# Block 0's k and q from row loads of their own, in a fused window attention and squared-ReLU feed-forward kernel

## The chip, the cores and the metric

The kernel runs on one core of a Trainium2 chip. A core has a matrix engine (TensorE, "PE" in the profile; its weight loads are "PEld"), a vector engine (VectorE, "DVE"), a scalar engine for activations (ScalarE, "ACT"), a general engine (GpSimd, "POOL"), and a queue engine (SyncE, "SP") that here issues nearly all DMA transfers. All five run programs of their own and wait for one another through semaphores. The metric is device time in microseconds (us), less is better; times of a kernel are the median of several runs.

## What is computed

```python
def _attn_ref(q, k, v):                      # each (8, 8, 576, 64): batch, heads, seq, head_dim
    scores = (1.0 / np.sqrt(64)) * np.matmul(q, k.transpose(0, 1, 3, 2))
    pos = np.arange(576)
    mask = np.abs(pos[:, None] - pos[None, :]) <= 32
    scores = np.where(mask, scores, -1000000000.0)
    scores = scores - np.max(scores, axis=-1, keepdims=True)
    attn = np.exp(scores)
    attn = attn / (np.sum(attn, axis=-1, keepdims=True) + 1e-09)
    return np.matmul(attn, v)

def _moe_ref(x, w_in, w_out, s, b):          # x (4608, 512), w_in (512, 2048), w_out (2048, 512)
    r = np.maximum(x @ w_in, 0.0)
    return (s * (r * r) + b) @ w_out
```

The attention's output, with the heads joined to rows of 512, is the feed-forward part's input x: 8 x 576 = 4608 tokens. Everything arrives as float32; the matrix products run in bfloat16.

## The kernel before

The 4608 tokens are 36 blocks of 128. A block's queries look at keys from 32 tokens before it to 32 behind it. For every block the attention makes a tile XT (the block's output, transposed), and the feed-forward part works on tiles of TILES: ten of 128 tokens, then thirteen of 256.

**Feed-forward.** For each tile, groups of 16 matmuls (L1188) make 512 columns of the hidden layer in the bank HT[0] or HT[1]; ACT or DVE takes the ReLU (L1197), DVE squares it into GT (L1216). Then four quarters of 4 matmuls each (L1238) add up the output in OUTP or PTPF, in turn; a quarter needs a quarter of w_out. The factor s and the constant b times w_out's column sums come in at L1252; those sums, cvec, are made once by PE from the whole of w_out (L1077).

**Attention.** Blocks 0 and 1 go through attend_light: scores for a group of four heads, in SC[0] or SC[1] (mask L800, products L810), a maximum for each query (L868), the same scores transposed (L800, L824) corrected by that maximum (L873, L875, L831, L836), one exponential (L892), the product with v (L845 to L852), scaling (L902, L904), a transpose back (L912) and the copy to XT. With NSPLIT = 1 block 0's two groups are heads 0 to 3 and heads 4 to 7, so that the first group needs only the first half of k and q. All other blocks go through attend: scores (L950), mask, minimum and exponential head by head (L962, L970), normalisation (L976 to L984), a transpose of the probabilities (by PE up to block 4, L1007, later by DMA), and the product with v (L1029 or L1046). A block j needs v tiles j and j + 1 (VE, VO).

**Where k and q come from.** For blocks 0 to 3 (WHOLE = 4) they come from whole-batch loads: "K0", "K1", "Q0", "Q1" (load_raw) bring batch 0 of k and q, four heads each, as 128 rows of 4608 bytes into RAW, which borrows space in GT. turn_raw casts them in four pieces each to FLAT, PE turns them by the permutation PERM (L691), and the banks are copied into TURN["K"] and TURN["Q"], from which keys(j) and qs(j) read. From block 4 on k and q come in tiles of 256 tokens ("k2", "q4" and so on, load_k and load_q), are cast (cast_kq) and transposed (kq_turn, L768).

**The weights.** w_in comes in four chunks i0 to i3 of 512 hidden columns, w_out in four chunks o0 to o3, each 1 MB in float32, into staging slots (SLOT: 0 to 3 lie in GT, 4 in OUTA), and each is cast in four pieces to WIN and WOUT (load_w, cast). v tiles are "v0", "v1" and so on (load_v, cast_v, make_vo).

**What sets the order.** All loads stand in one chain on SP, in the order of the string FIRST ("|" marks the block behind which the rest is put); each load stands behind the one before. Everything else is ordered by a planner (class _Plan): each operation is a node with a set of engines that it may run on, a cost, and a key; the planner walks through a model of the five engines and gives each engine the ready operation with the least key. What it finds is fixed in the program: an engine runs its list in that order and waits where an operand isn't there. Where PE would be idle early on, it puts in matmuls that compute nothing ("warm", L567; the first seven L571). akey(j) is the key of block j's attention, set by LEAD, L0 and LS; ckey gives the casts of loads their keys from their places in FIRST and from CB. LOOK, LOOK_GAP and LOOK_END would let an engine wait a moment for an operation that is due. FLEX, CSET, VSET, OSET and WSET say which engines may do which copies and casts, NSQ for how many blocks of tokens POOL may square.

```python
    FIRST = "Q0 Q1 K0 K1 i0 v0 v1 i1 i2 v2 i3 q4 v3 o0|k2 q5 v4 o1 o2 o3 v5||||"
    SLOT = dict(i0=0, i1=1, i2=2, i3=3, o0=0, o1=4, o2=1, o3=0)
    def akey(j):
        return 128 * j - min(LEAD, L0 + LS * j)
```

## Time and profile before

| | |
|---|---|
| median of 3 runs (lowest, highest) | 316.08 us (315.13, 317.0) |
| the profiled execution: its time | 316.29 us |
| its span from first to last instruction | 314.4 us |
| granted TensorE clock, mean over the span | 1.000 |
| DMA moved | 61.56 MB, mean 196 GB/s |
| most PE time: L1188 (hidden layer) | 147.1 us busy, 1472 matmuls |
| L1238 (output), the banks outp and ptp | 68.1 and 64.4 us busy |
| most DVE time: L1216 (square) | 82.0 us, 144 of 571 ns |
| most ACT time: L970 (exponential) | 113.3 us, 272 of 421 ns |
| most POOL time: L984 (normalisation) | 71.9 us, 64 of 1141 ns |

The profile is that of one execution. Its rows give an instruction's start, its duration, engine and source line, what it writes and reads, how many equal ones are merged, and, in brackets, how long the engine was idle before it and which event ended that. L645 and L650 are the lines of a helper that makes all copies and casts; there the names of the tiles tell them apart. Matmuls overlap in the pipeline, so PE's busy time is more than its work. Line 2 of the page cuts the span into 40 slices of 7.9 us, each with a digit for the tenths that were busy.

### The profile page before, as it was taken

To read this page: it belongs to the slowest core of one execution; us is meant where nothing else is said; L and a number is where in the kernel's file an instruction comes from. 1 tells how busy PE (TensorE), PEld (TensorE's weight loads), DVE (VectorE), ACT (ScalarE), POOL (GpSimd) and SP (SyncE) were. 2 spreads that over 40 slices of the span, in tenths; PEclk is the share of its full clock that TensorE was granted. 3 is DMA by queue.
4 is the path that set the end of the run, shared out by engine and by line. 5 is a ranking of instruction groups with operands and counts; after the bars stand their busy time and mean duration, and the time that the engine had idled before them with its cause. 6 is when DMAs were issued, how large, how long until landed. Compare 5 with 4: busy or idle time off the path is not lost.

```text
span 314.4 us, 10451 instructions
## 1 busy us (share of the span) xinstructions
PE 304.5 (97%) x4074; PEld 212.4 (68%) x4123; DVE 224.7 (71%) x903; ACT 228.9 (73%) x762; POOL 158.1 (50%) x208
## 2 busy tenths in 40 slices
PE   8999999999999999999999999999999999999996
PEld 3568867667777767767666766666667666667664
DVE  5579989997986777767767777777677776845332
ACT  6649895897898879777877787787778777854330
POOL 5567767667665455655545554555454645040000
DMA  7999999889999999999999999999999993241011
GB/s 293 356 333 257 322 289 236 225 177 206 217 216 208 206 198 188 195 220 228 178 190 191 251 178 198 225 228 183 201 219 260 177 141 69 69 99 43 30 67 67
DMA packets 156069, 61.56 MB, mean 196 GB/s; under 512 B 130164, under 2 KB 146932, under 8 KB 156020
## 3 DMA queue, kind: packets, MB, share of 16 engines
q1 hardware_dynamic: 156016, 60.90, 94.8%
q8 instruction: 32, 0.52, 0.7%
q14 instruction: 17, 0.14, 0.2%
q10 hardware_dynamic: 4, 0.00, 0.0%
HBM read 37.03 MB, written 9.44 MB: 148 GB/s over the span
## 4 chain that ended last, share of the span: by engine, by line
PE 70%; DVE 9%; DMA 8%; ACT 5%; SPq 3%; POOL 2%; issue 2%; DVEq 0%
PE ht L1188 28%; PE outp L1238 15%; PE ptp L1238 14%; DMA pts<-p 6%; DVE gt L1216 3%; PE sc L950 2%; ACT p L970 2%; POOL p L984 2%; DVE ss L962 2%; SPq L625 2%; DMA r32q<-in_q_dram 1%; PE tp L1046 1%; ACT r L1197 1%; PE sc L1238 1%; PE tp L768 1%
## 5 line engine op out<-in xcount | busy, mean ns | idle before, releaser
L1188 PE MATMUL ht<-xt,win 128*128 128x256 bf16 (+1 forms) x1472 | 147.1, 249 | 0.0
L1188 PEld LDWEIGHTS ht<-xt,win 128*128 128x128 bf16 x1472 | 118.0, 98 | 31.3 <-DVE xt L1063 0.2
L1197 ACT ACTIVATE r<-ht 128x512 bf16<-128x512 f32 x144 | 84.9, 590 | 45.5 <-PE ht L1188 44.1
L1216 DVE TENSOR_TENSOR gt<-r 128x512 bf16<-128x512 bf16 x144 | 82.0, 571 | 50.3 <-ACT r L1197 49.2
L970 ACT ACTIVATE p<-ss,mx 128x128 bf16<-128x128 f32 x272 | 113.3, 421 | 4.4 <-DVE mx L962 3.8
L984 POOL TENSOR_TENSOR p<-p,rc 128x512 bf16<-128x512 bf16 x64 | 71.9, 1141 | 57.0 <-DVE rc L979 57.0
L962 DVE CUSTOM_DVE_ANT_0 ss<-sc,mask 128x128 f32<-128x128 f32 x272 | 64.8, 281 | 7.2 <-PE sc L950 7.1
L1238 PE MATMUL outp<-wout,gt 128*128 128x512 bf16 (+1 forms) x265 | 68.1, 373 | 1.8 <-issue 1.0
L1238 PE MATMUL ptp<-wout,gt 128*128 128x512 bf16 x247 | 64.4, 379 | 2.2 <-issue 1.3
L970 ACT ACTIVATION_READ_ACCUMULATOR p<-ss,mx 128x1 f32 x272 | 52.1, 192 | 0.0
L1238 PEld LDWEIGHTS outp<-wout,gt 128*128 128x128 bf16 x288 | 27.0, 98 | 19.1 <-issue 0.4
L1238 PEld LDWEIGHTS ptp<-wout,gt 128*128 128x128 bf16 x272 | 25.4, 98 | 20.1
L645 POOL CAST kn<-r32k 128x512 bf16<-128x512 f32 x33 | 21.4, 675 | 25.4 <-DMA r32k<-in_k_dram 25.4
L645 POOL CAST ve<-v 128x512 bf16<-128x512 f32 x37 | 24.1, 652 | 19.5 <-PE av L1052 12.9
L1061 ACT COPY half<-tp 128x512 f32<-128x512 f32 x28 | 16.4, 585 | 15.3 <-PE av L1052 15.0
L645 POOL CAST qn<-r32q 128x512 bf16<-128x512 f32 x32 | 22.8, 714 | 7.9 <-DMA r32q<-in_q_dram 7.8
L962 DVE DVE_READ_ACCUMULATOR2_ANT mx<- 128x1 f32 x272 | 21.8, 80 | 0.0
L1063 DVE TENSOR_TENSOR xt<-av,half 128x512 bf16<-128x512 f32 x28 | 19.2, 684 | 1.5 <-ACT half L1061 1.4
L950 PEld LDWEIGHTS sc<-kt,qt 64*64 64x64 bf16 x768 | 10.7, 108 | 9.4 <-issue 8.3
L976 DVE TENSOR_SCALAR sm<-sm 128x8 f32<-128x8 f32 x34 | 7.1, 208 | 12.4 <-ACT p L970 12.4
L950 PE MATMUL sc<-kt,qt 64*64 64x64 bf16 (+1 forms) x768 | 14.2, 204 | 0.0
L1252 DVE SCALAR_TENSOR_TENSOR outs<-outp,scb,cvec 128x512 f32<-128x512 f32 (+1 forms) x18 | 13.0, 725 | 0.6 <-PE outp L1238 0.6
(159 smaller groups left out, 224.4 us busy)
## 6 DMA issues: line engine op xcount, KB each, us to landing
out_dram<-outs SPq DMA_DIRECT2D x35, 256.0 KB, 3.0
v<-in_v_dram SPq DMA_DIRECT2D x28, 256.0 KB, 5.8
r32q<-in_q_dram SPq DMA_DIRECT2D x28, 256.0 KB, 5.1
r32k<-in_k_dram SPq DMA_DIRECT2D x9, 512.0 KB, 5.2
gt<-in_moe_w_in_dram SPq DMA_DIRECT2D x4, 1024.0 KB, 10.0
gt<-in_moe_w_out_dram SPq DMA_DIRECT2D x3, 1024.0 KB, 9.0
v<-in_v_dram SPq DMA_DIRECT2D x8, 192.0 KB, 5.0
r32k<-in_k_dram SPq DMA_DIRECT2D x3, 448.0 KB, 5.1
```

The lines of the kernel that those rows point to most:

```text
L645: return e.tensor_copy(dst, src)
L950: r = e.matmul(SC[hh][64 * u:64 * u + 64, pr, x0:x1], lhsT=qq, rhs=kk, start=True, stop=True)
L962: lambda e, ss=ss, x=x, y=y, pr=pr, hh=hh: e.tensor_tensor_reduce(out=SS[ss][:, x, :], in0=SC[hh][:, pr, :], in1=MASK[kind][:, :], scale=- ...
L970: lambda e, ss=ss, x=x, y=y: e.activation(P[pb][:, y, :].rearrange("q (a p t) -> q a p t", a=2, t=2), spread(SS[ss][:, x, :]), AF.Exp, bia ...
L984: return e.tensor_tensor(P[pb][:, y0:y0 + 4, :], P[pb][:, y0:y0 + 4, :], RC[mb][:, y0:y0 + 4].unsqueeze(2).broadcast_to([128, 4, 128]), AL ...
L1061: add("act", lambda e: e.copy(HALF[hb][:, :], AV2[:, :]), 482, key + AVK, reads=[AV2N], writes=[("HALF", hb)])
L1063: add("dve", lambda e: e.tensor_tensor(XT[:, :, 128 * (j % NX):128 * (j % NX) + 128], AV[:, :, :], HALF[hb][:, :].rearrange("p (a b) -> p ...
L1188: r = e.matmul(hbank[:, nt * f:nt * f + nt], lhsT=WIN[:, kc, 128 * ft:128 * ft + 128], rhs=XT[:, kc, x0:x0 + nt], start=(kc == 0), stop=(k ...
L1197: return e.activation(R1[rb][:, :], hbank[:, :], AF.Relu, bias=0.0, scale=1.0)
L1216: return e.tensor_tensor(d, r, r, ALU.mult)
L1238: r = e.matmul(op_[:, 0:cn], lhsT=GT[:, g_, fc, :], rhs=WOUT[:, fc, c0:c0 + cn], start=(fc == 0), stop=(fc == 15))
L1252: add("dve", lambda e, ob=ob, op_=op_, c0=c0, cn=cn: e.scalar_tensor_tensor(OUTS[ob][:, 0:cn], op_[:, 0:cn], SCB[:, 0:1], CVEC[:, c0:c0 + cn],
```

## The change

Block 0 gets k and q by loads of its own, "k0" and "q0" (load_first): k's tokens 0 to 159, two tokens in a row of 512 bytes, 80 rows for each of 8 heads, and q's tokens 0 to 127 in rows of 256 bytes, 128 for each head. Each is cast in two halves to KQN, transposed by PE in ordinary 128-column transposes (8 for k, 4 for q) into the banks named in FBANK, and copied to the new tiles NEAR["k"] and NEAR["q"], which keys(0) and qs(0) read. The zeros before the first key are now put into NEAR["k"]. The four whole-batch loads stay, and TURN serves blocks 1 to 3. NSPLIT is 0, so block 0's two groups are now even and odd heads, and each needs all of NEAR.

FIRST is a new order, SLOT and TBANK (the banks of the whole-batch turns) are new assignments, and a number of planner constants and engine sets are different. TWEAK, by which single nodes could be moved, is empty.

```diff
--- before.py
+++ after.py
@@ -25,9 +25,10 @@
 START, RING, ISSUE, LAND = 800.0, 2400.0, 700.0, 1200.0
 PE_SLACK, STEADY = 400.0, 60000.0
 HOLD, DEFER, CHANGE = 400.0, 200.0, 97.0
-LOOK, LOOK_GAP, LOOK_END = 0.0, 50.0, 400000.0
+LOOK, LOOK_GAP, LOOK_END = 200.0, 20.0, 30000.0
 WARM, WARM_LOW, WARM_OVER, WARM_NS, WINDOW, WARM_END = 1.0, 0.66, 0.0, 225.0, 3413.0, 28000.0
 BANKS_ = (("HT", 1), ("HT", 0), "AV", "TP")
+TWEAK = {}
 HELD, HELD_END = {"dve": 100.0, "pool": 140.0}, 70000.0
 SHARED = ("FLAT", "WIN", "WOUT", "VE", "VO", "KQN", "GT", "M16", "SC1", "SC3")
 FILL, FILL_MIN, FILL_SHARE, FILL_NS = ("attn", "sums"), 400.0, 0.5, 220.0
@@ -153,6 +154,11 @@
 
     def order(self):
         for n in self.nodes:
+            if n.nid in TWEAK:
+                by, on = TWEAK[n.nid]
+                n.ready = by
+                if on and isinstance(n.eng, tuple) and on in n.eng:
+                    n.eng, n.cost, n.fn = on, n.cost[on], n.fn[on]
             n.left = len(n.deps)
             for m in n.deps:
                 m.users.append(n)
@@ -385,21 +391,23 @@
     NT = T // 128
     TILES = [128] * 10 + [256] * 13
     assert sum(TILES) == T
-    LEAD, L0, LS = 560, 470, 40
-    NSQ = 0
-    RELU, SQ = 700, 200
-    FIRST = "Q0 Q1 K0 K1 i0 v0 v1 i1 i2 v2 i3 q4 v3 o0|k2 q5 v4 o1 o2 o3 v5||||"
+    LEAD, L0, LS = 560, 470, 50
+    NSQ = 8
+    RELU, SQ = 500, 200
+    FIRST = "Q0 K0 k0 q0 v0 v1 Q1 K1 i0|i1 v2 i2 i3 o0 q4 v3 k2 q5 o1 o2 o3 v4 v5||||"
     ANY = ("act", "dve", "pool")
-    WSET = {"i": ("pool",), "o": ("act", "pool")}
-    VOP = 8
-    HSTEP, CB, VOK = 1.5, -400, -100
-    NFLEX, TAIL = 4, 2
+    WSET = {"i": ("pool", "act"), "o": ("act", "pool")}
+    VOP = 12
+    HSTEP, CB, VOK = 0.1, -300, 10
+    NFLEX, TAIL = 8, 2
     PDMA, KQDMA, AHEAD, GATE = 5, 11, 4, 5
-    CKEY, SKEY = 100, -9350
+    CKEY, SKEY = 300, -9250
     SPLIT1, SPKEY = True, -9000
-    SLOT = dict(i0=0, i1=1, i2=2, i3=3, o0=0, o1=4, o2=1, o3=0)
-    RAWNS, NSPLIT = 1450, 1
-    HC, HT_ = -9500, -50
+    SLOT = dict(i0=0, i1=1, i2=2, i3=3, o0=4, o1=0, o2=1, o3=2)
+    RAWNS, NSPLIT = 1450, 0
+    FBANK = {"q0": "A", "q1": "O", "k0": "T", "k1": "P"}
+    TBANK = {"Q0": "A00", "Q1": "101", "K0": "T00", "K1": "010"}
+    HC, HT_ = -400, 1
     WHOLE, LIGHT, CH, NDIV = 4, 2, S // 16, 6
 
     def FLEX(j):
@@ -413,10 +421,10 @@
 
 
     def CSET(j):
+        return ("pool",) if j >= 8 else ("pool", "act")
+
+    def VSET(j):
         return ("pool",) if j >= 4 else ANY
-
-    def VSET(j):
-        return ("pool",)
 
     def OSET(j, r0):
         return ANY if r0 == 0 and j < VOP else ("act", "dve")
@@ -462,6 +470,7 @@
                for x, g in (("K", 0), ("Q", 8))}
         FLAT = {"K": SSA[:, :, :, :].rearrange("p a b c -> p (a b c)").bitcast(BF16)[:, 0:CH * D],
                 "Q": PA[:, :, :, :].rearrange("p a b c -> p (a b c)")[:, 0:CH * D]}
+        NEAR = {"k": sb((128, NPAIR, 192), BF16, "kfirst"), "q": sb((128, NPAIR, 128), BF16, "qfirst")}
         TURN = {"K": sb((128, NPAIR, 32 + S), BF16, "kwt"), "Q": sb((128, NPAIR, S), BF16, "qwt")}
         MASKB = {m: sb((128, 128), BF16, "maskb") for m in ("mm", "fm")}
         MASKT = {m: sb((128, 128), BF16, "maskt") for m in ("mm", "fm")}
@@ -505,7 +514,7 @@
         add("dve", lambda e: e.memset(PART[:], 1.0 / 32.0), 150, K0 + 90, writes=["PART"])
         add("dve", lambda e: e.memset(ZERO[:], 0.0), 150, K0, writes=["ZERO"])
         add("dve", lambda e: e.memset(EPS[:], 1e-9 / 128.0), 150, K0 + 91, writes=["EPS"])
-        add("dve", lambda e: e.memset(TURN["K"][:, :, 0:32], 0.0), 150, K0 + 13, writes=["KPAD"])
+        add("dve", lambda e: e.memset(NEAR["k"][:, :, 0:32], 0.0), 120, K0 + 13, writes=["KPAD"])
         add("dve", lambda e: e.memset(V32[0][0:32, :], 0.0), 485, K0 + 12, writes=[("V32", 0, "lo")])
 
         def aff(dst, src, pat, base, cm, fill, rd, wr, key, cost=270):
@@ -679,9 +688,7 @@
                 move(("act", "dve", "pool"), {"act": 360.0, "dve": 220.0, "pool": 440.0},
                      flat[:, lo:lo + step], RAW[x][:, lo:lo + step], ckey_ + y + late,
                      [("RAW", x, half)] + stage(x, half), [("FLAT", x, y)])
-            banks = ([(TPF, "TP"), (HT[0], ("HT", 0)), (PTPF, "PTP")] if x == "K" else
-                     [(AVF, "AV"), (OUTP, ("OUTP", 0)), (HT[0], ("HT", 0))]) if half == 0 else [
-                         (HT[(i + (x == "Q")) % 2], ("HT", (i + (x == "Q")) % 2)) for i in range(3)]
+            banks = [PLACE[b] for b in TBANK[x + str(half)]]
             for i, (bank, res) in enumerate(banks):
                 at = 64 * (3 * n * half + n * i)
 
@@ -706,6 +713,48 @@
                 move(("act", "dve"), {"act": 110 + 0.73 * 64 * n, "dve": 20 + 73.0 * n}, dst, src,
                      tkey + 100 * (half == 0) + i + late, [res], [("TURN", x, half, i)])
 
+        PLACE = {"T": (TPF, "TP"), "P": (PTPF, "PTP"), "A": (AVF, "AV"), "O": (OUTP, ("OUTP", 0)),
+                 "0": (HT[0], ("HT", 0)), "1": (HT[1], ("HT", 1)),
+                 "S": (SC[0][:, :, :].rearrange("p a b -> p (a b)"), ("SC", 0)),
+                 "Z": (SC[1][:, :, :].rearrange("p a b -> p (a b)"), ("SC", 1))}
+
+        def load_first(x):
+            nat, kn = R32[x][0], KQN[x][0]
+            if x == "q":
+                src, rows, tok = q[0, :, 0:128, :].rearrange("h p d -> p h d"), 128, 1
+            else:
+                src, rows, tok = k[0, :, 0:160, :].rearrange("h (p t) d -> p h (t d)", t=2), 80, 2
+            wide = DM * tok
+            lastload[0] = add("sp", lambda e: [e.dma_start(
+                nat[0:rows, 0:wide].rearrange("p (h d) -> p h d", h=H), src)], 600, -LEAD - 3000,
+                writes=[("R32", x, 0, t) for t in range(2)], dsem=f"df{x}",
+                dtime=1250.0 if x == "q" else 1150.0, behind=lastload[0], ndesc=8 * rows)
+            for half in range(2):
+                w, r = wide // 2, ("R32", x, 0, 0)
+                a, b = nat[0:rows, w * half:w * half + w], kn[0:rows, w * half:w * half + w]
+                if x == "k":
+                    a = a.rearrange("p (h t d) -> p t h d", h=4, t=2)
+                    b = b.rearrange("p (t h d) -> p t h d", h=4, t=2)
+                move(("act", "dve", "pool"), {"act": 105 + 0.82 * w, "dve": 30 + 0.7 * w, "pool": 50 + w},
+                     b, a, -9900 + half, [r], [("KQN", x, 0, half)])
+                bank, res = PLACE[FBANK[x + str(half)]]
+                hb = halves(bank)
+
+                def turn(e, half=half, hb=hb):
+                    for i in range(2 * tok):
+                        at = w * half + 128 * i
+                        r = e.transpose(hb[:, i, 0:rows], kn[0:rows, at:at + 128], IDENT[0:rows, 0:rows])
+                    return r
+
+                add("pe", turn, 60 * 2 * tok, -9890 + half, reads=[("KQN", x, 0, half), "IDENT"], writes=[res])
+                out = NEAR[x][:, 2 * half:2 * half + 2, :]
+                got = hb[:, 0:2 * tok, 0:rows]
+                if x == "k":
+                    out = out[:, :, 32:192].rearrange("p g (c t) -> p g t c", t=2)
+                    got = got.rearrange("p (t g) c -> p g t c", g=2)
+                move(("act", "dve"), {"act": 110 + 0.73 * 2 * tok * rows, "dve": 20 + 1.0 * 2 * tok * rows},
+                     out, got, -9880 + half, [res], [("NEAR", x, half)])
+
         def load_k(c):
             s_ = c % NR["k"]
             load("k", 256 * c - 32, 256, 2, R32["k"][s_], ("R32", "k", s_, 0), 2 * c - 1,
@@ -772,13 +821,19 @@
             move(FLEX(j), {"dve": 603.0, "act": 892.0}, flat, TP[:, :, :], key, ["TP"], [wr])
 
         def turns(j, halves=(0, 1)):
-            return ["KPAD"] + [("TURN", x, half, i) for x in "KQ" for half in halves
+            if j == 0:
+                return ["KPAD"] + [("NEAR", x, half) for x in "kq" for half in halves]
+            return [("TURN", x, half, i) for x in "KQ" for half in halves
                                for i in range(3)]
 
         def keys(j, pr, hh, lo, hi):
+            if j == 0:
+                return NEAR["k"][64 * hh:64 * hh + 64, pr, lo:hi]
             return TURN["K"][64 * hh:64 * hh + 64, pr, 128 * j + lo:128 * j + hi]
 
         def qs(j, pr, hh, lo, hi):
+            if j == 0:
+                return NEAR["q"][64 * hh:64 * hh + 64, pr, lo:hi]
             return TURN["Q"][64 * hh:64 * hh + 64, pr, 128 * j + lo:128 * j + hi]
 
         def attend_light(j):
@@ -1120,6 +1175,9 @@
             if what[0] in "io":
                 load_w(what[0], int(what[1]))
             else:
+                if what in ("q0", "k0"):
+                    load_first(what[0])
+                    return
                 {"k": load_k, "q": load_q, "v": load_v,
                  "K": partial(load_raw, "K"), "Q": partial(load_raw, "Q")}[what[0]](int(what[1:]))
 

```

## The prediction

> **What bounds the kernel now.** I read the page's busy shares and slices first, then TensorE's rows in order of time, then the rows that waited for DMA, then DMA traffic in short stretches.
>
> ```profile
> PE 304.5 (97%) x4074; PEld 212.4 (68%) x4123; DVE 224.7 (71%) x903; ACT 228.9 (73%) x762; POOL 158.1 (50%) x208
> PE   8999999999999999999999999999999999999996
> DMA  7999999889999999999999999999999993241011
> ```
>
> PE is busy throughout, so the end time is set by how soon its work becomes useful. The first three slices of PE (7.9 us each) hold warm-up matmuls and small matmuls; DMA too is full from the first slice. So the front is a race: PE's work against the arrival of data. TensorE in order of time (start us, duration us, line, tiles, count):
>
> ```profile
> 1.32 3.17 PE L571 MATMUL ht<-ones 128*128 128x512 bf16 x7 [1.32 <-DVE nil L504]
> ...
> 10.33 0.39 PE L800 MATMUL sc<-maskb,ident 128*128 128x512 bf16 x1
> ...
> 23.25 1.07 PE L1188 MATMUL ht<-xt,win 128*128 128x128 bf16 x16
> ...
> 28.00 1.06 PE L1188 MATMUL ht<-xt,win 128*128 128x128 bf16 x16
> ...
> 34.31 0.81 PE L1238 MATMUL outp<-wout,gt 128*128 128x512 bf16 x3 [0.16 <-issue]
> ...
> 45.37 1.06 PE L1188 MATMUL ht<-xt,win 128*128 128x128 bf16 x16
> 46.35 1.05 PE L1077 MATMUL tp<-wout,ones 128*32 128x512 bf16 x16
> 47.56 0.81 PE L1238 MATMUL outp<-wout,gt 128*128 128x512 bf16 x3 [0.16 <-issue]
> ```
>
> Block 0's first scores start at 10.33, its first feed-forward matmuls (L1188) only at 23.25. Counted in groups (in the chain of waits a group of 16 at L1188 takes 0.89 us, a quarter of an output tile at L1238 0.86), PE had done 12 groups and 6 quarters by 45.37: 12 x 0.89 + 6 x 0.86 = 15.8 us. From 28 us on its rows follow each other almost without a hole: the list of waits gives PE 1.1 us of waiting from 23 to 70 us. What the weights did (POOL, the wait in brackets):
>
> ```profile
> 11.72 2.29 POOL L645 CAST win<-gt 128x512 bf16<-128x512 f32 x4 [2.32 <-DMA gt<-in_moe_w_in_dram]
> ...
> 24.25 2.48 POOL L645 CAST win<-gt 128x512 bf16<-128x512 f32 x4 [1.54 <-DMA gt<-in_moe_w_in_dram]
> ...
> 43.22 1.36 POOL L645 CAST wout<-gt 128x512 bf16<-128x512 f32 x2 [1.90 <-DMA gt<-in_moe_w_out_dram]
> ```
>
> w_in's chunks i0 and i3 are there at 11.72 and 24.25, w_out's last, o3, at 43.22, each with POOL waiting. DMA traffic in four stretches, 3 to 8, 11 to 12, 29 to 30 and 23.5 to 25 us:
>
> ```profile
> DMA packets 494, 2.00 MB, mean 401 GB/s; under 512 B 56, under 2 KB 56, under 8 KB 494
> DMA packets 1029, 0.26 MB, mean 259 GB/s; under 512 B 1029, under 2 KB 1029, under 8 KB 1029
> DMA packets 508, 0.24 MB, mean 238 GB/s; under 512 B 103, under 2 KB 507, under 8 KB 507
> DMA packets 522, 0.22 MB, mean 144 GB/s; under 512 B 485, under 2 KB 485, under 8 KB 520
> ```
>
> Long rows (the whole-batch loads, w) run at 401 GB/s; 256-byte rows at about 1029 packets a us; of the 508 packets in 29 to 30, 405 were k's 512-byte rows and 103 shorter. The last stretch is a slump.
>
> **The change, part by part.**
>
> *The new loads.* k0 is 8 heads x 80 rows of 512 bytes, 640 packets. 405 in 0.9 us (the 103 short ones took the other 0.1) is 450 a us: 1.4 us. From below, bytes alone: 0.33 MB at 401 GB/s, 0.8. q0 is 8 x 128 rows of 256 bytes, 1024 packets: 1.0 us by 11 to 12, 1.56 by the stretch 31 to 33 (1310 short packets in 2 us). Together 2.4 us, bounds 1.8 to 3.0. Nothing is taken away: all four whole-batch loads remain. [...]
>
> *Where they stand in SP's queue.* The order was Q0 Q1 K0 K1 i0 v0 v1 i1; it becomes Q0 K0 k0 q0 v0 v1 Q1 K1 i0 i1. So i0 moves past k0, q0, v0 and v1: 11.72 + 2.4 + (1792 short packets, 1.7 to 2.7) = 16 to 17. i1, i2 and i3 shift by the 2.4: i3 from 24.25 to 26.7. o0 is put ahead of q4 and v3, v4 behind o3. What is late next: v3, which block 2's last product needs (cast at 27.23 before, about 27.2 + 2.4 + 2.6 for o0's 1 MB at 401 GB/s = 32.2), and v4, which block 3 needs, behind o3.
>
> *Block 0's own path.* Q0 was cast at 4.42, the next whole-batch load at 5.86, so k0 is there at 5.86 + 1.4 = 7.3 and q0 at 8.3 to 8.9. Then a cast (0.43, row of 288 columns), 2 to 4 transposes (0.40, row L912), a copy (0.5, qwt rows), three hand-overs of 0.1: scores at 10.0, as before. Eight extra casts and copies, about 0.45 each, lie on three engines between 7 and 10 us, where DVE is busy 1.47 of 4 us (8 to 12); the 12 extra transposes stand where warm-up matmuls stand. Costed at nothing; without the cover 1.2 us on block 0's path. But now both groups of heads start at once; before, the second waited for K1's turn and its reduction stood at 15.55. From there the rows give: reductions 2 x 0.69 from 10.7; casts and subtractions 4 x 0.45; flip, copy, correction 0.22 + 0.26 + 0.39; exponential 0.60; product 0.5; reciprocal and scaling 0.59; transpose and copy 0.83; a dozen hand-overs at 0.1: 10.7 + 6.6 + 1.2 = 18.5, against 23.07. i0's four casts end at 16 to 17 + 1.25 to 2.5 (0.62 each on one or two engines), also near 18.5. So L1188 starts 4.7 us sooner.
>
> *What PE can do with it.* i3 comes at 26.7, cast by 28.0, just where before used it; blocks 0 and 1 can by then have three of four groups each, 5.3 us against 2.7 done before. After that PE runs out of data: blocks 0 to 2 allow 12 groups, o0 to o2 allow 3 quarters for two output banks, 6 quarters. That is the same 15.8 us that before had done at 45.37, and nothing more is to be had until o3 is cast. So the early start is given back, and o3 decides: 43.22 + 1.4 (k0) + 0 (q0 in, v4 out, equal sizes; -0.56 to +0.56) - 0.95 (the slump: o0 now has a buffer of its own, 0.22 MB at 401 GB/s is 0.55 of 1.5 us; 0 to -0.95) = 43.7. Its casts ran 43.22 to 45.47, 2.25 us; with ACT and POOL both free two each take 1.4. I take 1.4, since block 3's exponentials, which fill ACT then, can run while PE starves. 45.1 against 45.37: **-0.3** (-1.2 to +2.2).
>
> *Ahead in attention.* Block 4's p transposes (0.45 at 51.29) can fall into the starved time: **-0.45** (0 to -0.45).
>
> *Constants.* NSQ, NFLEX, VOP, CSET, VSET, WSET let POOL and ACT take squares, copies and casts of the first 8 to 12 blocks from DVE, which is busy 3.99 of 4 us from 40 to 44; PE is idle 0.47 and 0.11 us in 40 to 50 and 50 to 60: **-0.3** (0 to -0.58). LOOK, LS, RELU, SQ, CKEY and the bank letters reorder the same work: 0, with 0.6 either way.
>
> Sum: -1.05 on the profiled 316.29 (span 314.4, 1.9 around it), which lies 0.2 over the median of 316.08. **Forecast 315.0**, its own range 313.8 to 317.
>
> **The rivals.**
>
> *The early start is kept.* If o3 comes no later than before, the 4.7 us of PE time before 28 is not all lost: k0's 1.4 is the price, some 3.5 us stay: 312.6. For it: the slumps in 23.5 to 25 and 31 to 33, 144 and 213 GB/s, could close. Against it: DMA's slices are full to the end of the front and its bytes only grow.
>
> *The weights come late* (the other side). PE's order is fixed by the plan; where o3's quarter stands and the casts are not there, all behind it waits. o casts now rank behind block 3's attention. Worst terms: k0 1.5, q0 over v4 0.56, no slump gained, casts 2.25: 47.5, +2.2 us: 318.3. It decides from o3's cast ending after about 46.7. The idle stretches may also cost clock: the first seven fills took 3.17 us, 0.45 each, against 0.22 a matmul at L1238 later, so one cold spell costs 1.7 us: up to 320; price 319. [...]
>
> **How the numbers follow.** Forecast 0.48, early start kept 0.24, late weights 0.28. Predicted 315.0. The range 312.4 to 319.2 holds both rivals' prices and leaves their outer parts out, 2 in 10. A measurement of this kernel tells 0.5% (1.6 us) from no change: below 314.5 faster, above 317.7 slower. The forecast gives 0.18 faster, 0.27 same, 0.03 slower; the second all faster; the third 0.05 same, 0.23 slower: 0.42, 0.32, 0.26.
>
> **What would show it.** In the changed profile: L1188's first row near 18.5 (if after 21, block 0's path was mis-costed); w_in's last cast waiting for DMA near 26.7; holes on PE between 30 and 45 in front of L1188 or L1238; w_out's last wait ended by DMA at 43 to 45; L1077 near 46. If PE shows no holes there and o3 is earlier than 43, the second case holds. If L1077 stands after 48, the third. A change that sits after 60 us would make the whole reasoning wrong.

## The result, and the profile after

The changed kernel takes 317.32 us (median of 13 runs, 315.74 to 321.67), the kernel before beside it 315.50 (13 runs, 314.61 to 317.88). The ratio is 1.005, 95% interval 1.003 to 1.007: slower by half a per cent, where 315.0 and a small gain were forecast. Medians here and below are of all executions; ratios leave out those that took over 1.5% longer than the quickest of their kernel (one of the thirteen here, 321.67). The profiled execution of the changed kernel took 318.23 us, 0.9 over its median, with a span of 316.5 and a granted clock of 1.0, so its rows show the loss somewhat enlarged.

From the page of the kernel after: busy time of the engines, and PE's and DMA's slices of 7.9 us.

```profile
PE 308.7 (98%) x4130; PEld 212.1 (67%) x4130; DVE 223.0 (70%) x906; ACT 235.8 (75%) x772; POOL 153.8 (49%) x203
PE   7999989999999999999999999999999999999996
DMA  8999999899999999999999999999999992241011
```

As before, PE is full and says little; ACT has taken over work from POOL. PE in order of time (start us, duration us; L855 was L800, L967 was L912, L1246 was L1188, L1296 was L1238, L1132 was L1077):

```profile
10.29 0.39 PE L855 MATMUL sc<-maskb,ident 128*128 128x512 bf16 x1
...
18.73 0.38 PE L855 MATMUL sc<-maskb,ident 128*128 128x512 bf16 x1 [0.56 <-ACT kwt L659]
...
19.41 0.40 PE L967 MATMUL tp<-ident,xn 128*128 128x128 bf16 x4
...
21.69 1.07 PE L1246 MATMUL ht<-xt,win 128*128 128x128 bf16 x16
...
22.84 1.07 PE L1246 MATMUL ht<-xt,win 128*128 128x128 bf16 x16
...
26.93 1.06 PE L1246 MATMUL ht<-xt,win 128*128 128x128 bf16 x16
27.82 0.39 PE L967 MATMUL tp<-ident,xn 128*128 128x128 bf16 x4
...
29.14 2.92 PE L1246 MATMUL ht<-xt,win 128*128 128x128 bf16 x48
...
44.85 1.06 PE L1246 MATMUL ht<-xt,win 128*128 128x128 bf16 x16
47.02 1.02 PE L1296 MATMUL outp<-wout,gt 128*128 128x512 bf16 x4 [1.11 <-POOL wout L654]
...
48.34 1.05 PE L1132 MATMUL tp<-wout,ones 128*32 128x512 bf16 x16
```

The feed-forward part starts 1.6 us sooner than before (21.69 against 23.25), but has only three groups done by 28 us, as before, and at 47.02 it stands in a hole of 1.11 us that the kernel before does not have. Whom it waits for is on POOL (in brackets the wait and what ended it):

```profile
17.61 1.18 POOL L654 CAST win<-gt 128x512 bf16<-128x512 f32 x2 [4.90 <-DMA gt<-in_moe_w_in_dram]
20.09 1.18 POOL L654 CAST win<-gt 128x512 bf16<-128x512 f32 x2 [1.31 <-DMA gt<-in_moe_w_in_dram]
23.88 1.92 POOL L654 CAST win<-gt 128x512 bf16<-128x512 f32 x3 [2.05 <-DMA gt<-in_moe_w_in_dram]
26.37 2.29 POOL L654 CAST win<-gt 128x512 bf16<-128x512 f32 x4 [0.57 <-DMA gt<-in_moe_w_in_dram]
...
45.70 1.18 POOL L654 CAST wout<-gt 128x512 bf16<-128x512 f32 x2 [2.97 <-DMA gt<-in_moe_w_out_dram]
```

i0 to i3 and o3 all come off DMA, o3 2.5 us later than before (45.70 against 43.22).

Progress says it in one table. It counts the weight loads of L1246 and L1296 up to a time and gives each its step (0.056 us in a tile of 128, 0.109 in one of 256, 0.216 for an output matmul: a group of 16 takes 0.89, a quarter 0.86). Each row is one profiled execution; the last five are experiments told below.

```
feed-forward matmul time done (us) by    24    28    36    44    48    52    60    72   100 us
before                                  0.7   2.7   8.6  14.6  17.6  20.2  25.7  35.5  58.9
after                                   1.8   2.7   8.0  14.3  16.7  19.3  24.4  32.9  56.8
again (the kernel after, repeated)      1.8   2.7   8.4  14.1  15.9  18.2  22.9  32.5  55.0
near_thin                               1.8   2.7   8.8  15.3  17.8  20.5  25.5  35.0  58.5
long_rows                               1.8   2.6   8.0  13.9  16.7  19.4  24.6  34.2  57.9
mixed                                   1.8   2.7   8.0  14.7  16.7  20.1  24.6  34.1  58.5
w_first                                 1.8   2.7   8.0  15.2  17.6  19.7  23.7  33.3  56.6
```

The lead of 1.1 us at 24 is gone at 28; 0.9 is lost by 48, 1.3 by 60, 2.6 by 72 and 2.1 by 100, as much as the two spans differ (314.4 and 316.5). So the loss is made in the front, the hole being about half of it. The table counts feed-forward matmuls alone, so a row also moves when attention work is put earlier or later: long_rows has no hole (below) and stands at 16.7 at 48 like after. The last column is the safest.

### The profile page after: what moved, and what is told of

It reads as the page before. It is cut to its first block, busy times and chain, and to the rows that moved or that the text cites. A ratio compares the mean times of both kernels' runs of the same rounds, so it can differ in the third digit from the quotient of the medians.

```text
span 316.5 us, 10525 instructions
## 1 busy us (share of the span) xinstructions
PE 308.7 (98%) x4130; PEld 212.1 (67%) x4130; DVE 223.0 (70%) x906; ACT 235.8 (75%) x772; POOL 153.8 (49%) x203
## 4 chain that ended last, share of the span: by engine, by line
PE 63%; DMA 17%; SPq 6%; POOL 5%; DVE 4%; ACT 3%; issue 1%
PE ht L1246 28%; PE outp L1296 14%; PE ptp L1296 13%; DMA pts<-p 4%; DMA gt<-in_moe_w_out_dram 4%; DMA r32q<-in_q_dram 3%; SPq L634 3%; DMA gt<-in_moe_w_in_dram 3%; POOL p L1039 2%; PE sc L1005 2%; DMA r32k<-in_k_dram 2%; DVE ss L1017 2%; ACT p L1025 1%; DMA v<-in_v_dram 1%; SPq L1053 1%; PE tp L1101 1%
## 5 line engine op out<-in xcount | busy, mean ns | idle before, releaser
L1246 PE MATMUL ht<-xt,win 128*128 128x256 bf16 (+1 forms) x1472 | 147.0, 249 | 0.2 <-ACT r L1255 0.2
L1246 PEld LDWEIGHTS ht<-xt,win 128*128 128x128 bf16 x1472 | 117.9, 98 | 31.3 <-ACT r L1255 0.7
L1039 POOL TENSOR_TENSOR p<-p,rc 128x512 bf16<-128x512 bf16 x63 | 70.7, 1142 | 55.2 <-DVE rc L1034 55.2
L1296 PE MATMUL outp<-wout,gt 128*128 128x512 bf16 (+1 forms) x288 | 72.0, 373 | 1.1 <-POOL wout L654 1.1
L1296 PE MATMUL ptp<-wout,gt 128*128 128x512 bf16 x272 | 69.9, 379 | 0.0
L1296 PEld LDWEIGHTS outp<-wout,gt 128*128 128x128 bf16 x288 | 27.0, 98 | 20.3 <-ACT wout L659 1.3
L1296 PEld LDWEIGHTS ptp<-wout,gt 128*128 128x128 bf16 x272 | 25.3, 98 | 20.5 <-issue 0.4
L654 POOL CAST ve<-v 128x512 bf16<-128x512 f32 x37 | 25.0, 676 | 18.8 <-PE av L1107 11.0
L654 POOL CAST qn<-r32q 128x512 bf16<-128x512 f32 (+1 forms) x32 | 20.8, 651 | 13.2 <-DMA r32q<-in_q_dram 13.2
L1005 PEld LDWEIGHTS sc<-kt,qt 64*64 64x64 bf16 x768 | 10.7, 108 | 9.9 <-issue 8.7
L1031 DVE TENSOR_SCALAR sm<-sm 128x8 f32<-128x8 f32 x34 | 6.4, 189 | 12.4 <-ACT p L1025 12.4
L1005 PE MATMUL sc<-kt,qt 64*64 64x64 bf16 (+1 forms) x768 | 14.2, 204 | 0.0
```

The lines of the kernel that those rows point to most:

```text
L654: return e.tensor_copy(dst, src)
L1005: r = e.matmul(SC[hh][64 * u:64 * u + 64, pr, x0:x1], lhsT=qq, rhs=kk, start=True, stop=True)
L1039: return e.tensor_tensor(P[pb][:, y0:y0 + 4, :], P[pb][:, y0:y0 + 4, :], RC[mb][:, y0:y0 + 4].unsqueeze(2).broadcast_to([128, 4, 128]), AL ...
L1246: r = e.matmul(hbank[:, nt * f:nt * f + nt], lhsT=WIN[:, kc, 128 * ft:128 * ft + 128], rhs=XT[:, kc, x0:x0 + nt], start=(kc == 0), stop=(k ...
L1296: r = e.matmul(op_[:, 0:cn], lhsT=GT[:, g_, fc, :], rhs=WOUT[:, fc, c0:c0 + cn], start=(fc == 0), stop=(fc == 15))
```

## The experiments

Ratios are to the kernel before, run beside each on the same chip; its median was 315.19 to 315.68 in the first three series and 317.32 on the chip of the last, where only runs of that series are compared.

**pad_front, pad_mid, pad_late: the added transfers alone, at three places in the kernel before.** Two loads that nothing reads, seven eighths of k0's packets and all of q0's, outside the plan: by the prediction's prices 2.2 us of transfer (7/8 of 1.4, and 1.0), by what the two took in the kernel after 2.1 (7/8 of 1.0, and 1.2):

```diff
-    FIRST = "Q0 Q1 K0 K1 i0 v0 v1 i1 i2 v2 i3 q4 v3 o0|k2 q5 v4 o1 o2 o3 v5||||"
+    FIRST = "Q0 Q1 K0 K1 xk xq i0 v0 ..."      pad_front
+    FIRST = "... i3 xk xq q4 v3 o0|k2 ..."     pad_mid
+    FIRST = "... o1 o2 o3 xk xq v5||||"        pad_late
+        src = k[0, 0:7, 0:160, :].rearrange("h (p t) d -> p h (t d)", t=2)
```

> The kernel before, with two loads that nobody reads put behind K1: seven eighths of k0 (560 rows of 512 bytes) and q0 (1024 rows of 256 bytes); its plan does not know of them. Theory A (w_out's last chunk o3 comes late because of the added DMA, and PE runs out of work): o3's cast starts 2.0 to 2.5 us after before's 43.2, PE stands idle in front of the column sums or the last output quarters, and the time rises by 1.0 to 2.0 us over before (316.5 to 317.5). Theory B (the new plan's order of PE work costs the time, the added DMA is hidden): within 0.5 us of before.

Measured: 321.98 us, ratio 1.0197 [1.0166, 1.0228], far over any of the sums. The table of stretches (PE, PEld, DVE, ACT, POOL busy, then the granted clock, DMA share, GB/s) shows why:

```profile
16.00:18.00 2.00, 1.65 (x35) 0.94 (x32) 0.54 (x2) 1.15 (x2) 2.00 (x5) 1.00 1.10 386
18.00:20.00 2.00, 1.26 (x19) 0.75 (x21) 1.97 (x8) 0.67 (x2) 1.15 (x3) 0.64 1.01 377
20.00:26.00 6.00, 6.00 (x54) 3.00 (x52) 2.44 (x7) 1.17 (x4) 4.82 (x9) 0.50 1.15 331
26.00:32.00 6.00, 6.00 (x92) 4.84 (x92) 3.78 (x24) 3.97 (x12) 3.85 (x7) 0.50 0.95 254
32.00:34.00 2.00, 2.00 (x52) 1.85 (x51) 1.24 (x7) 1.52 (x8) 0.00 (x0) 0.95 1.22 247
```

PE was idle 1.1 of the 4 us from 16 to 20, and from 19 to 32 us its clock was half. All six runs have a mean clock of 0.978 to 0.984. So this run prices the transfers together with a cold spell, and it took two more to part them.

> The kernel before with two loads that nothing reads (7/8 of k0's bytes and all of q0's, in their packet sizes, some 2.2 us of the DMA engines) put behind i3, so that block 0's and block 1's loads and all of w_in land as before and only w_out, k2, q5 and v5 are later. Theory A: o3's first cast goes from 43.22 to about 45.3, the hole ahead of the first matmuls of chunk 3 opens, and the time rises by 1 to 1.5 us (ratio 1.003 to 1.005). Theory B (what was lost in the padded front was the clock's spell at half speed alone): with the clock at 1.0 throughout, the time stays within 0.3 us.

Measured: 318.92, ratio 1.0122 [1.0077, 1.0168], profiled at a clock of 1.0, o3's first cast at 47.02. The spell was not all of it: 2.2 us of transfers cost 3.7 us here. Nor was o3: PE's wait for its casts is 0.27 us (at 45.77) and 0.29 (at 48.84), and the largest, 1.36 at 32.72, is for block 2's probabilities (L1020): POOL normalises them, behind a reciprocal on DVE, which stands there behind v3's cast; that cast waited 0.68 us for DMA. So a load put early makes several of the later ones late, each for its own reader.

> The kernel before with the same two unread loads put behind o3, where only v5 follows. Theory A (what counts is how late o3 is): o3's first cast stays at 43.2 and the time within 0.5 us (ratio 1.000 to 1.0015). Theory B (the bytes cost wherever they are put, because block 4's and block 5's loads are as tight): the time rises by 1 to 2 us (ratio 1.003 to 1.006).

Measured: 317.09, ratio 1.0055 [1.0023, 1.0087]: Theory A's "within 0.5 us" missed, Theory B's 1 to 2 us holds: bytes behind o3 cost as well. Which of the later loads is the tight one this run does not show well: in its profiled execution PE waits 1.20 us at 59.86 for the casts of q of blocks 6 and 7 (L781), but that execution took 319.71 and was late from 24 us on, so this, and o3's 45.56 in it, tell little of the median.

**before_less: is there slack the other way?** The first w_out load moves a quarter of its bytes, and all four casts read that quarter:

```diff
+            few = 1 if (which, c) == ("o", 0) else 4
-            ... e.dma_start(w32[:, :, :], src)], 500, -LEAD - 900,
+            ... e.dma_start(w32[:, 0:few, :], src[:, 0:few, :])], 500, -LEAD - 900,
-                cast(WSET[which], w32[:, g, :], ...
+                cast(WSET[which], w32[:, g % few, :], ...
```

> The kernel before with the same cut of o0 (256 KB in place of 1 MB, the output differs). It is the other half of the pair: what is 768 KB of transfer worth in the kernel before? Theory A: o3's first cast, at 43.22, moves about 1.9 us sooner, and the time falls by 0.5 to 1.5 us (ratio 0.995 to 0.998), as in the kernel after or somewhat less. Theory B: the loads are no bound, and the time stays within 0.3 us (ratio 0.999 to 1.001).

Measured: 315.47, ratio 1.0008 [0.9988, 1.0029], o3's cast at 43.66. 768 KB less, at 401 GB/s some 1.9 us, buys nothing. o3 did not come sooner either (43.66 against 43.22), so the run does not say what a sooner o3 would be worth. More to carry costs at once, less gains nothing: by this pair the kernel before just meets its due times.

**after_less: the same cut in the kernel after.**

> The kernel after, but the first w_out load (o0) moves only its first quarter, 256 KB in place of 1 MB, and all four casts of o0 read that quarter (the output differs); every instruction's place in the order stays. Theory A (the added k0 and q0 make every later load late, and o3's cast is what the matmuls wait for at 47 us): o3's first cast starts about 1.9 us sooner (43.8 in place of 45.70), the hole of 1.11 us ahead of L1296 goes, and the time falls by 1.2 to 1.8 us to about 315.8 (ratio to the kernel before about 1.001). Theory B (the new order of PE's work costs the time, whenever the loads land): the time stays within 0.3 us of the kernel after's 317.3.

Measured: 316.28, ratio 1.0019 [0.9989, 1.0048], in size what Theory A said, but not in its way: o3's first cast stayed at 45.52, and the hole shrank to 0.45 us only because PE came to it 0.7 us later. k2 and q5 landed 2 us sooner (32.2 and 33.3 against 34.2 and 35.3, by their packets in the trace), o3 did not:

```profile
45.52 1.38 POOL L655 CAST wout<-gt 128x512 bf16<-128x512 f32 x2 [2.20 <-DMA gt<-in_moe_w_out_dram]
```

So bytes alone were not what held o3. SP's own queue shows what may have (start us, duration of the issue):

```profile
22.95 1.02 SPq L634 DMA_DIRECT2D v<-in_v_dram  x1
24.01 5.90 SPq L634 DMA_DIRECT2D r32k<-in_k_dram  x2
29.95 0.52 SPq L634 DMA_DIRECT2D r32q<-in_q_dram  x1
30.57 3.92 SPq L605 DMA_DIRECT2D gt<-in_moe_w_out_dram  x3
```

This is the kernel after: SP stood 5.90 us at k2's two issues, 5.17 of them at the first, which began with 2,626 packets issued and not yet landed and ended with 669; o1 to o3 stand behind it. The engines ran dry towards its end: 133 GB/s from 28 to 30. In after_less the same stall only began sooner, 22.57, took 6.85 and ended at 29.42 against 29.91, with 125 GB/s from 28 to 30. But its o1 to o3 were all issued by 32.4, 2 us sooner than after's, and o3 landed no sooner, so the stall is not the whole of it. What stops SP there the run does not show.

**long_rows: fewer packets, same bytes.** v3 and q5 read 128 rows of 2 KB:

```diff
+                    if (x, t0) in (("v", 352), ("q", 640)):
+                        rows = src[b, :, :, :].rearrange("h s d -> (h s d)")[0:65536]
+                        got.append(e.dma_start(dst[:, :], rows.rearrange("(p c) -> p c", p=128)))
+                        continue
```

> The kernel after, but v3 and q5 read their 256 KB as 128 rows of 2 KB in place of 1,024 pieces of 256 B (the output differs; bytes, order and plan stay): 1,792 packets fewer, some 1.8 us of the DMA engines less, about as much as the 768 KB left out of o0 in the run called after_less, which did not bring o3's cast forward (45.52 against 45.70). Theory C (SP's issue stands still at k2 because too many packets are outstanding, 2,626 at 24.19 us, and the engines then run dry): k2's issue takes under 2 us in place of 5.17, the slump of 104 to 216 GB/s at 29 to 32 us goes, o3's first cast starts at 43.5 or sooner, the hole ahead of L1296 goes, and the time falls by 0.8 to 1.5 us (ratio to the kernel before 1.000 to 1.0025). Theory A (bytes or the engines' time): as in after_less, o3's cast within 0.5 us of 45.6 and a time at 1.002 or above.

Measured: 315.92, ratio 1.0005 [0.9976, 1.0034]. SP's queue, then o3's first cast, then PE where after has its hole:

```profile
22.95 1.03 SPq L635 DMA_DIRECT2D v<-in_v_dram  x1
24.02 3.19 SPq L638 DMA_DIRECT2D r32k<-in_k_dram  x2
27.25 2.12 SPq L635 DMA_DIRECT2D r32q<-in_q_dram  x1
29.48 2.61 SPq L605 DMA_DIRECT2D gt<-in_moe_w_out_dram  x3
```

```profile
43.55 1.17 POOL L658 CAST wout<-gt 128x512 bf16<-128x512 f32 x2 [0.56 <-DMA gt<-in_moe_w_out_dram]
```

```profile
45.21 1.06 PE L1250 MATMUL ht<-xt,win 128*128 128x128 bf16 x16
46.10 1.03 PE L1300 MATMUL outp<-wout,gt 128*128 128x512 bf16 x4
```

k2's issues last 3.19 in place of 5.90 (not under 2, as Theory C had it), o3's first cast starts at 43.55, and no hole stands ahead of the matmuls. 28 to 30 us carried 232 GB/s against 133. Packets counted here, as Theory C says: by estimate 0.7 to 1.8 us of engine time was saved (2,048 rows of 256 bytes at 1,029 to 655 a us, the rates from 11 to 12 and from 31 to 33 us in the kernel before, less 256 of 2 KB at 401 GB/s), no more than in after_less (1.9), but here it was o3 that moved. The run does not part SP's stall from the packets' own time, though: v3's 896 packets fewer stand ahead of the stall, q5's 896 behind it, directly ahead of o1.

**mixed, o1_first, w_first: the same loads in other orders.**

```diff
-    FIRST = "... i3 o0 q4 v3 k2 q5 o1 o2 o3 v4 v5||||"
+    FIRST = "... i3 o0 v3 o1 q4 k2 o2 q5 o3 v4 v5||||"    mixed
+    FIRST = "... i3 o0 q4 v3 o1 k2 o2 q5 o3 v4 v5||||"    o1_first
+    FIRST = "... i3 o0 v3 o1 o2 o3 q4 k2 q5 v4 v5||||"    w_first
```

> The changed kernel with q4, k2 and q5 put behind o3 in the order of loads. Theory A: o3's cast starts at 41 to 42 in place of 45.7, the hole of 1.1 us on PE goes, and the time falls by 1.5 to 2.5 us to 315 to 316. Theory B: 317 to 318, as the changed kernel, or slower, since block 4's k and q come later.

Measured: 319.12, ratio 1.0101 [1.0070, 1.0131]. o3's casts came 5 us sooner and the hole went (17.6 by 48 us, level with before), but by 60 two us are missing, as Theory B allowed: PE waits 0.41 us at 48.11 for block 4's scores (L1005) and 0.68 at 57.50 for the casts of q of blocks 6 and 7 (L817), which stand on POOL behind a k cast that waited 3.15 us for DMA. (A q load is 128 tokens, a k load 256; the loads behind FIRST, k3, q6, q7 and so on, follow in the same chain.)

> The kernel after with the loads behind o0 in the order v3 o1 q4 k2 o2 q5 o3 v4 v5 (after: q4 v3 k2 q5 o1 o2 o3 v4 v5); all bytes and packets stay. Theory C: with long packets between the short ones SP stands still while there is still a megabyte under way, the engines do not run dry, o3's first cast starts at 41 to 43.5 in place of 45.70, the 1.11 us hole goes, and the time falls by 1 to 1.5 us to about 316 (ratio 1.000 to 1.002), unless k2 and q5, at 38 to 43 in place of 34 and 35, come late for block 4 as in the run called w_first. Theory A (bytes): o3 as late as before within 0.7 us, since as many bytes precede it; ratio 1.004 to 1.006.

Measured: 317.29, ratio 1.0060 [1.0032, 1.0087], the kernel after's own time, as Theory A had it. In the profiled execution o3's cast came at 43.92, a little behind Theory C's range, and the hole was gone. But that execution, 316.25, was the quickest of its twelve and lost nothing, so its trace does not say why the median did.

> The kernel after with o1 between v3 and k2 and o2 between k2 and q5 (o0 q4 v3 o1 k2 o2 q5 o3). Theory C: SP stands still at o1 in place of k2, with the same 2,600 packets ahead, until o0's last packet has landed near 29, the engines run dry all the same at 29 to 31, and o3's cast is at 44.5 to 45.7; time within 0.6 us of the kernel after's (ratio 1.003 to 1.006). Theory A (order alone counts, as it did in w_first): o3's cast comes 1.5 us sooner or more (k2's and q5's 2.2 us partly behind it), ratio about 1.002.

Measured: 318.79, ratio 1.0108 [1.0071, 1.0145]. SP stood 5.46 us at o1 as Theory C said, o3's cast came at 46.58, later than the 45.7 allowed, and the time is 1.5 us over the kernel after. Its largest wait on PE is again for q of blocks 6 and 7: 1.57 us at 59.34, for a cast on ACT that waited 1.44 for DMA.

Three orders, none better: with all loads in, something comes late, o3 or the k and q behind it.

**before_mixed: the mixed order in the kernel before** (FIRST "... i3 v3 o0|o1 q4 o2 k2 o3 q5 v4 v5||||").

> The kernel before with the loads behind i3 in the order v3 o0 o1 q4 o2 k2 o3 q5 v4 v5 (before: q4 v3 o0 k2 q5 v4 o1 o2 o3 v5). Theory C: the slump of 196 to 258 GB/s that the kernel before has from 22 to 34 us goes as well, o3's first cast starts 2 us sooner or more (41 in place of 43.22). If the kernel before is bound by o3's cast the time falls by up to 0.9 us (ratio 0.997); if it is not (before_less, 1.0008, says so) the time stays within 0.3 us, or rises by up to 1 us where block 4's q4 and k2 come late.

Measured: 316.91, ratio 1.0033 [1.0005, 1.0061], the last of the cases named. o3's first cast came at 41.28, 1.9 us sooner, and the kernel was slower: o3 alone does not set the time there either. PE waits 1.33 us at 56.05 for the casts of q of blocks 6 and 7 (L768); in the kernel before it comes to the same matmuls at 55.66 and waits for nothing:

```profile
55.66 0.61 PE L768 MATMUL tp<-ident,qn 128*128 128x128 bf16 x8
```

**no_near and near_old: the two halves of the change.** no_near is the kernel after without k0 and q0 (block 0 reads TURN again); near_old has k0, q0 and block 0's new path under the constants, sets, slots and nearly the order of before.

```diff
-    FIRST = "Q0 K0 k0 q0 v0 v1 Q1 K1 i0|i1 ..."
+    FIRST = "Q0 K0 v0 v1 Q1 K1 i0|i1 ..."                  no_near
+    FIRST = "Q0 K0 k0 q0 Q1 K1 i0 v0 v1 i1 ..."            near_old
```

> The changed kernel's constants, order and buffers without the loads k0 and q0; block 0 reads the whole-batch tiles. Theory A: o3's cast starts 2.0 to 2.5 us sooner than 45.7, and the time is 315 to 316 although block 0 starts its feed-forward work later. Theory B: the plan's constants are the cost, so it stays at 317 or more.

Measured: 321.12, ratio 1.0143 [1.0103, 1.0184]. Some of its runs had a spell at half clock like pad_front's (23 to 33 us in the profiled one); three at a mean clock of 1.0 took 318.41, 318.69 and 320.90. Theory A's 315 to 316 missed. Under the new constants and order, then, k0 and q0 do what they are for: without them it is 1 us slower or more. It prices nothing else, since in this order Q1 and K1, which block 0 now has to wait for, stand behind v0 and v1, and the planner made another plan.

> The loads k0 and q0 and block 0's new path with all constants, engine sets and buffers of the kernel before; the order of loads is before's with K0, k0, q0 behind Q0. Theory A: the added DMA is the same, o3 is late by 2.0 to 2.5 us, so 316.5 to 318. Theory B: no loss without the new constants: 314.5 to 315.5.

Measured: 322.09, ratio 1.0199 [1.0172, 1.0226] at full clock, o3's first cast at 45.84. Some 1.5 us are missing by 60 us, but 3 more are lost after 180 us, in a plan that came out otherwise there; so only its front can be used, and it agrees with the pads.

**near_thin and again: the kernel after with its new loads made cheap, and itself.** k0 moves half its bytes as 80 long rows, q0 as 128; order and instructions stay:

```diff
+            flat = (q if x == "q" else k)[0, :, :, :].rearrange("h s d -> (h s d)")[0:rows * wide // 2]
-                nat[0:rows, 0:wide].rearrange("p (h d) -> p h d", h=H), src)], 600, -LEAD - 3000,
+                nat[0:rows, 0:wide // 2], flat.rearrange("(p c) -> p c", p=rows))], 600, -LEAD - 3000,
-                a, b = nat[0:rows, w * half:w * half + w], kn...
+                a, b = nat[0:rows, 0:w], kn...
```

> The kernel after, but k0 moves half its bytes as 80 rows of 2 KB (after: 640 pieces of 512 B) and q0 half of its bytes as 128 rows of 1 KB (after: 1,024 pieces of 256 B), and both casts of each read the same half (the output differs); instructions, order and plan stay. It takes some 1.4 of the 2.2 us of these two loads and 1,456 of their 1,664 packets away. Theory L (the loss is these transfers): every later load lands 1 to 1.5 us sooner, and the time falls by 1 to 1.6 us against the run called again, to a ratio of 1.000 to 1.002. Theory P (the loss is the plan and its added work): within 0.4 us of again.

> The kernel after, unchanged. All theories: ratio 1.003 to 1.007 as in its first runs; o3's first cast at 45.0 to 46.4, a hole of 0.3 to 1.3 us ahead of the first matmuls that use it.

Measured on one chip: near_thin 316.53, again 317.60, 1.07 us apart by their medians. By their ratios to the kernel before, 0.9964 [0.9934, 0.9995] and 1.0027 [0.9993, 1.0062], it is 0.6%, some 2 us, with intervals that just touch. again's profiled execution has the hole of after, larger: 1.95 us, with o3's cast at 46.79. near_thin, POOL, then PE:

```profile
16.33 1.17 POOL L654 CAST win<-gt 128x512 bf16<-128x512 f32 x2 [4.93 <-DMA gt<-in_moe_w_in_dram]
...
25.04 2.29 POOL L654 CAST win<-gt 128x512 bf16<-128x512 f32 x4 [0.56 <-DMA gt<-in_moe_w_in_dram]
...
43.20 1.17 POOL L654 CAST wout<-gt 128x512 bf16<-128x512 f32 x2 [1.86 <-DMA gt<-in_moe_w_out_dram]
```

```profile
20.41 1.07 PE L1247 MATMUL ht<-xt,win 128*128 128x128 bf16 x16
...
43.56 1.06 PE L1247 MATMUL ht<-xt,win 128*128 128x128 bf16 x16
44.52 1.02 PE L1297 MATMUL outp<-wout,gt 128*128 128x512 bf16 x4
```

Every row of the front stands 1.3 us sooner than after's, o3's 2.5, where the kernel before has it; the hole is gone and progress is within 0.5 us of before's from 48 us on. Theory L holds: with the same plan and the same matmuls, the loss goes with the transfers. SP's stall at k2 is shorter too, 4.08 us in place of 5.90. Its second ratio says more than was asked: on this chip near_thin is quicker than the kernel before by some 0.4%.

**back_first: block 0's back-transpose ahead of block 1's first scores.**

```diff
-                            key + h_, reads=["B" + kind, "IDENT"] + need, writes=[("SC", hh)])
+                            key + h_, reads=["B" + kind, "IDENT"] + need, writes=[("SC", hh)],
+                            after=backs[0:1] if j == 1 else [])
```

> The kernel after with block 1's first scores made to wait, in the plan, for block 0's back-transpose (L967), so that this goes to PE ahead of them. The forecast put block 0's first matmul with w_in at 18.5 us and it was at 21.69, because PE's order has 2.3 us of block 1's scores ahead of it. Theory O (that order is what held it): the first matmul starts at 19.5 to 20.5. What it is worth: Theory L (the loads bound the front): nothing, within 0.4 us of again. Rival (the start counts in full): 1 to 1.5 us faster than again.

Measured: 317.76, ratio 1.0021 [0.9988, 1.0053], level with again. But in its profiled execution (326.72 us) the mask matmuls (L855) took 0.61 to 0.63 us in place of 0.39 from 12.92 on, though the granted clock reads 1.0, and the first feed-forward matmul still stood behind all of block 1's scores, at 29.96. Whether an earlier start is worth anything was therefore not tried; inconclusive.

## Why the prediction was wrong

**What held.** *The new loads*, in sum: k0 and q0 kept the engines from 5.6 to 7.8 us, 2.2 against 2.4 predicted. The parts were off in opposite ways, and that the sum came out is luck. From 5.7 to 6.1 us, where k0's packets had the engines nearly to themselves, 272 landed in 0.4 us at 344 GB/s, not 450 a us at 230. So by estimate k0's 640 cost 1.0 us, not 1.4, and q0 the rest, 1.2, not 1.0. The bound from below, 0.8 us for k0's bytes at 401 GB/s, was the nearer figure; the stretch at 29 to 30 us, from which the 450 was read, was no measure for k0's rows at 5.7 to 6.1. *SP's queue*: i0 at 17.61 (16 to 17), i3 at 26.37 (26.7). *Block 0's path* up to the scores: 10.29 (10.0, and 10.33 before), with the extra casts and transposes in it. *The cap*: up to the hole PE had done exactly 12 groups and 6 quarters, and then waited for o3.

**Where it failed: o3's arrival.** The term was 43.22 + 1.4 + 0 - 0.95 = 43.7; it measured 45.70, 46.79 in again, 2.0 us or more too late. The slump of 0.95 was to be recovered because o0 has a buffer of its own. It was not: it came back at 28 to 32 us (133 and 215 GB/s), where SP had stood still at k2 (5.90 us) with over 2,000 short packets out, and fewer packets brought o3 to 43.55 (long_rows). The other 1.0 us no run splits; q0 against v4, put at nothing because their bytes are equal, was never tested alone. near_thin gives the price of the whole: 1.4 us of transfer less (an estimate: 2.2 less 0.295 MB at 401 GB/s) brought 2.5 us of o3 and 1.1 to 2 us of time, so these two loads near the front cost o3 more than their own length.

**Block 0's start was mis-costed**, by the mark that was set (after 21): 21.69 against 18.5. The sum followed block 0's own chain and left out PE's fixed order. The chain's scaling was done at 18.44 in DVE's rows, where the sum has about 17.6 (18.5 less 0.83 for transposes and copy and a hand-over). The transposes then stood behind the first of four groups of block 1's scores, which waited 0.56 us for K1's turn (19.41); XT was copied by 20.43 in ACT's rows, and the other three groups stood ahead of L1246 until 21.69. And "5.3 us against 2.7 done before" by 28 was 2.7: block 1's rows became ready only after its back-transpose at 27.82, because Q1 and K1 stand behind k0, q0, v0 and v1, and i2's cast at 23.88 allowed block 0 no third group sooner. The hand-overs at 0.1 us, 1.2 of that sum, no row shows: in the kernel before, up to 60 us, an engine that had waited for another started 0.03 to 0.08 us after it (medians by pair of engines, as PE to ACT 0.04, DVE to POOL 0.08). In the forecast's own sum this failure costs nothing, since the early start was given back there anyway; no run tested that.

**Ahead in attention** (-0.45) and **constants** (-0.3) stay open: with the new loads cheap, near_thin's progress in the table is no better than before's, but its ratio to the kernel before on the same chip, 0.9964 [0.9934, 0.9995], is a gain of some 1.1 us, about the whole sum's 1.05. They were not measured singly.

**The rivals.** *The weights come late* was right: casts done at 46.88, past its point of 46.7; L1132 at 48.34, past the mark of 48. Its price, 318.3 to 320, was too high against 317.32, for it took the worst of each term. Its cold spell was not in the profiled executions of after; of the thirteen, twelve had a mean clock of 1.0 and one, 321.67 us, 0.973. pad_front and no_near show how near it lies. That idling slows PE, on which its 1.7 us rests, was the author's estimate and not shown: the rows have the first seven fills at 0.45 us each, not the reason, and of the two spells at half clock pad_front's followed 1.1 us of idling in 4, no_near's none in the 4 before it. *The early start is kept* fell with o3. The range held the time, and the sign was wrong.

**What is not settled.** That the loss goes with the two new loads' transfers is shown by near_thin. The path is not shown whole: the hole at o3 is one place where late loads come out, 1.11 of some 2 us in after's trace, and not the only one. w_first and o1_first lose at the q of blocks 6 and 7 (0.68 and 1.57 us), before_mixed too (1.33) with o3 sooner than ever, pad_mid at v3 (1.36). What share of after's loss each has was not measured alone. No variant was found that beats the kernel before with all of its data loaded.

## What to carry to other kernels

Where a chain of loads already runs full and just meets its due times, price an extra load by what stands last in the chain, at the same length or more, and not by the work that it makes ready sooner. Test for slack both ways, with a load that nothing reads and with one cut short: here 2.2 us more cost 1.9 to 3.7 where the clock held, and 1.9 us less gained nothing. The last in the chain is not the only one to price: every load behind the new one has a reader that may stand waiting (here v3's, 1.36 us in pad_mid, and that of q of blocks 6 and 7, 0.68 to 1.57). Count packets as well as bytes: here 1,792 packets fewer at equal bytes brought o3 from 45.70 to 43.55, and with two loads in rows of 256 bytes under way SP stood 5.90 us at k2's issues while DMA fell to 133 GB/s (28 to 30 us).

## What the hardware showed that was not expected

A cold spell did not have to follow idle time here, and PE's being busy did not end it at once. In no_near the clock was halved from about 23 to 33 us (stretch, then PE, PEld, DVE, ACT, POOL busy, granted clock, DMA share, GB/s):

```profile
18.00:22.00 4.00, 4.00 (x49) 2.04 (x48) 1.12 (x4) 3.06 (x7) 2.41 (x5) 1.00 1.05 405
22.00:28.00 6.00, 5.76 (x83) 3.47 (x83) 2.88 (x11) 2.98 (x6) 2.49 (x5) 0.60 1.08 245
28.00:33.00 5.00, 5.00 (x76) 4.23 (x69) 3.22 (x21) 3.01 (x11) 3.51 (x7) 0.50 0.87 215
```

PE was busy 4.00 of the 4 us before it. In pad_front PE had idled 1.1 us in 4, was then busy 6.00 of 6.00 us in two stretches running and kept half clock through both, some 13 us in all. What starts such a spell and what ends it is open: the kernel after has much the same matmuls and kept 1.0 in its profiled execution.

An issue on SP took 5.17 us with 2,626 packets out at its start, 2,048 of them rows of 256 bytes (k2's first, in the kernel after); q5's, right behind it, took 0.52 with 1,113 out. The kernel before has it too: 3.33 us at o0's issue with 2,267 out.

Rows of 512 bytes ran at 344 GB/s from 5.7 to 6.1 us in the kernel after, and at 238 from 29 to 30 in the kernel before, where 103 of the 508 packets were shorter.
